# Means of squares of the second and third token group: block transposes on VectorE in place of matmuls, PSUM read out by ScalarE

## The chip, the cores and the metric

The kernel runs on one core of a Trainium2 chip. The metric is the device time of one execution in microseconds (us). The engines are named as in the profile: PE (TensorE's matmuls), PEld (its weight loads), DVE (VectorE), ACT (ScalarE), POOL (GpSimd) and SP (which only issues DMAs here). Each engine takes its instructions in program order; semaphores make one engine wait for another.

## What is computed

Attention without softmax, a normalisation of its result, and then two matrix products with a nonlinear function between them:

```python
kv = np.einsum('bhsd,bhse->bhde', k, v)                            # (8, 8, 64, 64)
out = np.einsum('bhsd,bhde->bhse', q, kv)                          # (8, 8, 576, 64)
rms = np.sqrt(np.mean(out * out, axis=-1, keepdims=True) + 1e-06)
x = (out / rms * g_norm)            # then (B,H,S,D) -> (B*S, H*D): 4608 x 512
h = x @ w_in                        # 4608 x 2048
g = h * erf(softplus(h))
result = g @ w_out                  # 4608 x 512
```

Everything is float32. What matters here is the third and the fourth line: a mean of squares over the 64 values of a head, for each token.

## The kernel before

**Groups and units.** The 8 batches of 576 tokens are worked on as nine groups of 512 tokens: the first 512 tokens of each batch are a group (T = 0 to 7), and the last 64 tokens of all batches together are the ninth. The hidden dimension of 2048 is cut into 16 units of 128. One loop (L1156) goes through n = 0 to 31, which are the units of the first group (n = 0 to 15) and of the second (n = 16 to 31); a second loop (L1323) does the other groups, four units at a time. While the units of one group are computed, the attention of the next one is prepared between them: that of the second group (T = 1) beside n = 0 to 15, and that of the third (T = 2, `FIRST`) beside n = 16 to 31. The attention of later groups is written differently (`paired`, L542) and the change only takes some of its lines out into functions of their own.

**Pairs.** A group's attention is done for two heads at a time, so in four pairs p = 0 to 3. `attention(T, p)` (L404) returns the steps of one pair and `pieces_of` (L1028) puts them into the iterations: every iteration has the places 3, 0, 1 and 2, in this order in time. For the second group the pairs begin at units f = 3, 6, 9 and 12, for the third at f = 0, 4, 8 and 12. Steps of a pair before the change:

- `visit` (in iteration f+1, place 1; for p = 0 of the second group f+2, place 3): PE multiplies q with k^T v of the pair into a PSUM tile of two banks, `at` (L427, L437), and k^T v of the *next* pair into another part of the same tile (L432). ACT squares the result `o` into `qT` (L445).
- `halve` and `keep_tail` (f+2, place 3): DVE splits the squares into an upper and a lower part (L459, L460; not for the first pair of the second group), copies the 64 last tokens' result into `x_last` (L448), and brings k^T v of the next pair into SBUF: each half of it is copied to the other half of the partitions (L371, two copies of 64 partitions) and added (L372).
- `mean` (f+2): PE multiplies the squares with a matrix of 1/64 (L470, L471; L476 for that first pair), so that the mean stands in every partition of its head, and ACT forms the reciprocal root over 128x512 values: Ln, Exp, Square (L482 to L484). ACT has to load its tables for Ln and Exp before (L114) and those for Softplus after them (L117), 1.28 us each.
- `norm` (f+3, place 0): DVE refines the root (L490, L493) and multiplies `o`, still in PSUM, with it (L502); `turn` (L347) transposes q of the next pair.
- `split` (f+4, place 0; third group): ACT and DVE cut x into the three parts that the next group's products take (L713, L716, L719).

For the last pair of the third group (p = 3, visit in n = 29), mean, norm and split come in `held_sums` (L1110), in n = 32, where the two loops meet. There PE also multiplies four units that were held back (`g_held`, L1098); DVE makes their parts (L716, L719) after `add` (L753) and `gates` (L1082) of unit n = 30, and PE waits for each part. The next unit's `n_ps` takes the PSUM tile that ACT has to empty first (L1216).

**What else is in the queues.** Beside n = 0 to 15 the weights, which come as 64-bit numbers, are made into float32: ACT takes the lower words (L271), DVE joins them in four operations (`w_join`, L281 to L292). The join of a pair of units has to be done before their first product (L1201). Beside n = 16 to 31 DVE and ACT cut all weights into three parts (`w_upper` L737, `w_lower` L740 and L743) and write them to memory. Every iteration also has, on ACT, the copy of the products out of PSUM (L1214, L1216) and Softplus (L1230), and on DVE `add` (second group, L753) and the product of h and erf (L1082).

**Two engines on one PSUM bank** take turns in program order, two readers too: DVE's first copy of `x_last` started at 46.16 us, when ACT's square of other columns of the same tile (45.55 us, 0.58 long) had ended, though PE had written these columns by 41.9 us.

Of the kernel before, what the change touches and what calls it, by code (L numbers as in the profile page):

```python
# [70 lines left out]
def kernel(  # L71
# [293 lines left out]
    def kv_kept(T, p, at, cols=kv_cols):  # L365


        kv = kv_of(T, p).rearrange("p (a e) -> p a e", a=2)
        other = other_tile(1)[:, 0]
        for i in range(2):  # L370
            nc.vector.tensor_copy(out=other[rows_of[i]], in_=at[rows_of[1 - i], ::-1, cols])  # L371
        nc.vector.tensor_tensor(out=kv, in0=at[:, :, cols], in1=other, op=ALU.add)  # L372
# [30 lines left out]

    def attention(T, p):  # L404
# [3 lines left out]
        halves = T > 1 or (T == 1 and p > 0)  # L408
# [7 lines left out]

        def square_tile(name):
            return qt_tile(name)[:, 0:G]

        def visit():  # L420
# [24 lines left out]
            nc.scalar.activation(two(st["sq"]), st["o"], AF.Square)  # L445

        def keep_tail():
            nc.vector.tensor_copy(  # L448
                out=x_last[:, p, T * R : T * R + R], in_=st["at"][:, 1, 2 * P : 2 * P + R]
            )  # L450
            kv_kept(*then, st["at"])
            if both:
                kv_kept(then[0], 1, st["at"], more_cols)

        def halve():
            sq = st.pop("sq")
            hi = st["hi"] = attp.tile([P, G], FP32R, name="sq_hi", tag="rms_r")
            lo = st["lo"] = attp.tile([P, G], FP32R, name="sq_lo", tag="sq_lo")
            nc.vector.tensor_copy(out=hi, in_=sq)  # L459
            nc.vector.tensor_tensor(out=lo, in0=sq, in1=hi.bitcast(FP32), op=ALU.subtract)  # L460

        def mean(table=True):
            ms = st["ms"] = st["at"][:, :, 2 * P : 4 * P]
            parts = [(ms[:, a], a) for a in range(2)]
            if halves:


                hi, lo = two(st.pop("hi")), two(st.pop("lo"))
                for ps, a in parts:
                    nc.tensor.matmul(ps, lhsT=mean_w, rhs=hi[:, a], start=True, stop=False)  # L470
                    nc.tensor.matmul(ps, lhsT=mean_w, rhs=lo[:, a], start=False, stop=True)  # L471
                u = square_tile("u")
            else:
                u = st.pop("sq")
                for ps, a in parts:
                    nc.tensor.matmul(  # L476
                        ps, lhsT=mean_w.bitcast(FP32), rhs=two(u)[:, a], start=True, stop=True
                    )
            r = attp.tile([P, G], FP32, name="rms_r", tag="rms_r")
            exp_ln_table()  # L480
            st["u"], st["r"] = u, r
            nc.scalar.activation(two(r), ms, AF.Ln, bias=eps_col)  # L482
            nc.scalar.activation(r, r, AF.Exp, scale=-0.5)
            nc.scalar.activation(u, r, AF.Square)  # L484
            if table:
                softplus_table()

        def norm():
            ms, u, r = (st.pop(name) for name in ("ms", "u", "r"))
            nc.vector.scalar_tensor_tensor(  # L490
                out=two(u), in0=ms, scalar=EPS, in1=two(u), op0=ALU.add, op1=ALU.mult
            )
            nc.vector.scalar_tensor_tensor(  # L493
                out=u, in0=u, scalar=3.0, in1=r, op0=ALU.subtract, op1=ALU.mult
            )
            if T < FIRST:
                if T not in xT:
                    xT[T] = wide.tile([P, KC, G], FP32, name="xT", tag="ab"[T])
                x = xT[T][:, p, :]
            else:  # L500
                x = st["x"] = x_new.tile([P, G], FP32, name="x", tag="x")
            nc.vector.scalar_tensor_tensor(  # L502
                out=two(x),
                in0=st.pop("o"),
                scalar=gm_col,
                in1=two(u),
                op0=ALU.mult,
                op1=ALU.mult,
            )

        def split_upper():
            if T >= FIRST:
                upper(st["x"], x_forms[T][0][:, p])

        def split_lower():
            if T >= FIRST:
                lower(st.pop("x"), *(form[:, p] for form in x_forms[T]))

        def split():
            split_upper()  # L520
            split_lower()
# [14 lines left out]
        pieces = (first_, (visit, loads), (halve, keep_tail) if halves else (keep_tail,))  # L536
        return (*(partial(chain, *group) for group in pieces), mean, partial(chain, norm, then_), split)
# [4 lines left out]
    def paired(T, p):  # L542
# [76 lines left out]
        def small(name):  # L619
            t = twice[name] = attp.tile([P, 2 * BLOCKS], FP32, name=name, tag=name)  # L620
            return t

        def block_sums():


            total = small("ms")
            for n in range(2):
                t = attp.tile([P, G], FP32, name="sq_t", tag=("rms_r", "sq_lo")[n])
                nc.vector.transpose(out=t, in_=twice["x"][n])
                nc.vector.tensor_reduce(  # L630
                    out=total[:, n * BLOCKS : n * BLOCKS + BLOCKS],
                    in_=t.rearrange("p (c d) -> p c d", c=BLOCKS),
                    axis=AX.X,
                    op=ALU.add,
                )

        def across():


            total, other = twice["ms"], small("ms_other")  # L640
            for n in range(4):
                rows, beside = (slice(32 * k, 32 * k + 32) for k in (n, n ^ 1))
                nc.scalar.copy(other[rows], total[beside])
            nc.vector.tensor_tensor(out=total, in0=total, in1=other, op=ALU.add)

        def root():
            total, r, u = twice["ms"], small("rms"), small("rms_u")
            exp_ln_table()
            nc.scalar.activation(r, total, AF.Ln, bias=eps_col)
            nc.scalar.activation(r, r, AF.Exp, scale=-0.5)  # L650
            nc.scalar.activation(u, r, AF.Square)
            softplus_table()

        def spread():


            total, r, u = (twice[name] for name in ("ms", "rms", "rms_u"))
            nc.vector.scalar_tensor_tensor(
                out=u, in0=total, scalar=EPS, in1=u, op0=ALU.add, op1=ALU.mult
            )  # L660
            nc.vector.scalar_tensor_tensor(
                out=u, in0=u, scalar=3.0, in1=r, op0=ALU.subtract, op1=ALU.mult
            )
            for n in range(2):
                nc.vector.transpose(
                    out=twice["x"][n].rearrange("p (c d) -> p c d", c=BLOCKS),
                    in_=u[:, n * BLOCKS : n * BLOCKS + BLOCKS].unsqueeze(2).to_broadcast([P, BLOCKS, 32]),
                )
# [783 lines left out]
```

## Time and profile before

| what | value |
|---|---|
| median of three runs | 884.97 us (883.99 to 885.11) |
| the profiled execution | 885.1 us, of which 883.2 us are its span |
| PE busy in the span | 875.2 us (99%), 4874 matmuls |
| DVE, ACT busy | 752.5 us (85%), 558.4 us (63%) |
| 51 to 116 us (second group's pairs 1 to 3): PE, DVE, ACT busy | 64.78, 61.80, 43.51 of 65.00 us |
| 129 to 216 us (third group's pairs): PE, DVE, ACT busy | 87.00, 75.78, 64.73 of 87.00 us |
| 216 to 250 us (`held_sums` and after): PE, DVE, ACT busy | 33.45, 29.87, 23.09 of 34.00 us |
| granted PE clock | 1.00 in all of these stretches |

The span is what the profiler's instructions cover; some 1.9 us of the execution lie around it. PE's time is modelled for the ends of its matmuls, so the starts are what to read: a row of matmuls without a gap between the starts is PE at work. DVE is nearly as full as PE while the second and third group are prepared, so an operation more on DVE may or may not be covered, and this has to be read place by place. In the views, each row has the start, the length, the engine and the line, and in brackets how long the engine had stood idle before it and what released it.

### The profile page before, as it was taken

The numbers are of one execution on the slowest core, as the hardware profiler recorded it, in microseconds if no ns is written. First come the engines' busy times: TensorE is split into PE (matmuls) and PEld (weight loads), VectorE is DVE, ScalarE is ACT, GpSimd is POOL, SyncE is SP. The second block draws the span as 40 slices with busy tenths as digits, with TensorE's granted clock in tenths as the row PEclk, the third lists the DMA queues.
The fourth block names the chain that finished last, engine by engine and source line by source line (L and its number), as shares of the span: only waits on it lengthen the run. The fifth ranks groups of instructions, "written<-read, shape, count | busy, mean of one in ns | idle before, by whom it ended". The sixth has DMA issues, their size and how long they took to land.

```text
span 883.2 us, 13302 instructions
## 1 busy us (share of the span) xinstructions
PE 875.2 (99%) x4874; PEld 656.1 (74%) x4874; DVE 752.5 (85%) x1107; ACT 558.4 (63%) x789; POOL 4.7 (1%) x14
## 2 busy tenths in 40 slices
PE   8999999999999999999999999999999999999998
PEld 4444456656788888888888888888888888888887
DVE  5889978899999898989898989898979797966667
ACT  5977677777775657565665647474757575755552
POOL 2000000000000000000000000000000000000000
PEclk9999999999999999999999999999999999999999
DMA  9967427989799997998799879998897778778861
GB/s 289 292 220 225 137 75 277 345 306 351 257 346 409 332 353 250 391 327 345 233 381 357 337 240 351 361 341 288 281 352 283 287 288 346 291 274 336 314 255 48
DMA packets 136929, 259.89 MB, mean 294 GB/s; under 512 B 78816, under 2 KB 87264, under 8 KB 136864
## 3 DMA queue, kind: packets, MB, share of 16 engines
q1 hardware_dynamic: 136128, 258.09, 81.8%
q10 hardware_dynamic: 544, 0.82, 0.3%
q8 instruction: 39, 0.64, 0.3%
q14 instruction: 26, 0.21, 0.1%
q0 software_dynamic: 192, 0.13, 0.0%
HBM read 224.40 MB, written 34.60 MB: 293 GB/s over the span
## 4 chain that ended last, share of the span: by engine, by line
PE 94%; DVE 2%; DMA 2%; ACT 1%; issue 0%; SPq 0%; DVEq 0%
PE n_ps L778 49%; PE m_ps L778 24%; PE o_ps L834 9%; PE h_ps L1201 5%; DMA w_out_parts<-w_out 1%; PE diag_ps L578 1%; PE at_ps L583 1%; PE n_ps L1098 1%; PE warm_ps L982 1%; DMA w_raw<-in_moe_w_out_dram 1%; PE at_ps L432 0%; PE at_ps L437 0%; PE o_ps L1098 0%; DVE w_in_sb L292 0%; DVE w_e L287 0%; PE off_ps L578 0%
## 5 line engine op out<-in xcount | busy, mean ns | idle before, releaser
L778 PE MATMUL n_ps<-w_out_parts,g_forms 128*128 128x512 f32 (+1 forms) x936 | 229.9, 388 | 0.2 <-DMA w_out_parts<-w_out 0.2
L778 PE MATMUL n_ps<-x_forms,w_in_parts 128*128 128x512 f32 x896 | 222.6, 390 | 0.0
L778 PEld LDWEIGHTS n_ps<-w_out_parts,g_forms 128*128 128x128 f32 x936 | 175.1, 188 | 36.5 <-DMA w_out_parts<-w_out 0.6
L778 PEld LDWEIGHTS n_ps<-x_forms,w_in_parts 128*128 128x128 f32 x896 | 167.4, 188 | 38.3 <-issue 3.9
L753 DVE TENSOR_TENSOR h<-m_ps,h 128x512 f32<-128x512 f32 x116 | 78.5, 686 | 66.1 <-PE m_ps L778 63.9
L1363 ACT ACTIVATE s<-h 128x512 f32<-128x512 f32 x112 | 69.2, 632 | 88.1 <-DVE h L753 88.1
L778 PE MATMUL m_ps<-w_out_parts,g_forms 128*128 128x512 f32 x464 | 123.9, 389 | 0.0
L1358 ACT ACTIVATE h<-n_ps 128x512 f32<-128x512 f32 x112 | 66.7, 596 | 85.6 <-PE n_ps L778 83.2
L778 PE MATMUL m_ps<-x_forms,w_in_parts 128*128 128x512 f32 x448 | 119.7, 389 | 0.0
L778 PEld LDWEIGHTS m_ps<-w_out_parts,g_forms 128*128 128x128 f32 x464 | 87.1, 188 | 18.1
L778 PEld LDWEIGHTS m_ps<-x_forms,w_in_parts 128*128 128x128 f32 x448 | 84.1, 188 | 17.5
L753 DVE TENSOR_TENSOR e<-m_ps,e 128x512 f32<-128x512 f32 x116 | 80.1, 691 | 13.8 <-PE m_ps L778 3.4
L834 PE MATMUL o_ps<-w_out_sb,h_sb 128*128 128x512 f32 x192 | 86.8, 595 | 0.0
L713 ACT ACTIVATE g_forms<-h 128x1024 fp32r<-128x1024 f32 x58 | 60.8, 1061 | 39.0 <-PE m_ps L778 20.8
L719 DVE SCALAR_TENSOR_TENSOR g_forms<-g_forms 128x1024 fp32r<-128x1024 f32 x58 | 71.1, 1225 | 2.0
L716 DVE TENSOR_TENSOR g_forms<-h,g_forms 128x1024 fp32r<-128x1024 f32 x58 | 70.5, 1216 | 0.5 <-ACT g_forms L713 0.4
L1412 DVE TENSOR_TENSOR h<-h,s 128x1024 f32<-128x1024 f32 x56 | 65.9, 1216 | 0.0
L834 PEld LDWEIGHTS o_ps<-w_out_sb,h_sb 128*128 128x128 f32 x192 | 35.5, 190 | 40.2 <-issue 38.0
L748 DVE SCALAR_TENSOR_TENSOR e<-n_ps,e 128x512 f32<-128x512 f32 (+1 forms) x89 | 59.8, 672 | 3.5 <-PE n_ps L778 3.5
L1201 PE MATMUL h_ps<-xT,w_in_sb 128*128 128x512 f32 x128 | 57.9, 596 | 1.3 <-DVE w_in_sb L292 1.2
L117 ACT ACT_TABLE_LOAD x43 | 55.2, 1283 | 0.8
L1386 ACT ACTIVATE s<-s 128x1024 f32<-128x1024 f32 x50 | 50.6, 1054 | 0.3
(166 smaller groups left out, 935.3 us busy)
## 6 DMA issues: line engine op xcount, KB each, us to landing
w_out_parts<-w_out SPq DMA_DIRECT2D x116, 768.0 KB, 7.2
w_in_parts<-w_in SPq DMA_DIRECT2D x112, 768.0 KB, 6.8
w_in<-w_new SPq DMA_DIRECT2D x16, 768.0 KB, 4.9
k_sb<-in_k_dram SPq DMA_DIRECT2D x32, 288.0 KB, 6.1
v_sb<-in_v_dram SPq DMA_DIRECT2D x31, 288.0 KB, 5.8
w_raw<-in_moe_w_in_dram SPq DMA_DIRECT2D x16, 512.0 KB, 6.2
w_raw<-in_moe_w_out_dram SPq DMA_DIRECT2D x8, 1024.0 KB, 5.0
out_dram<-e SPq DMA_DIRECT2D x32, 256.0 KB, 4.1
```

The source lines that it names most:

```text
L117: nc.scalar.preload_act_table_set("softplus")
L713: nc.scalar.activation(high, x, AF.Copy, scale=1.0 + 2.0**-13)
L716: nc.vector.tensor_tensor(out=low, in0=x, in1=high.bitcast(FP32), op=ALU.subtract)
L719: nc.vector.scalar_tensor_tensor(out=both, in0=low.bitcast(FP32), scalar=SHIFT, in1=high.bitcast(FP32), op0=ALU.mult, op1=ALU.add,)
L748: nc.vector.scalar_tensor_tensor(out=out_, in0=ps, scalar=scale, in1=out_, op0=ALU.mult, op1=ALU.add)
L753: nc.vector.tensor_tensor(out=out_, in0=ps, in1=out_, op=ALU.add)
L778: nc.tensor.matmul(ps[:, cols], lhsT=weights(form, k), rhs=moving(form, k)[:, cols], start=(form == forms[0] and k == 0), stop=(form == fo ...
L834: nc.tensor.matmul(o_ps[j], lhsT=g[:, j * P : j * P + P], rhs=one(w_out_sb, f), start=(f == 0), stop=last,)
L1201: nc.tensor.matmul(plain[i], lhsT=blocks_of(one(w_in_sb, i % FC))[:, c], rhs=xT[T][:, c, :], start=(c == 0), stop=(c == KC - 1),)
L1358: nc.scalar.activation(h[:, i], n_ps, AF.Copy, scale=SHIFT - 1.0)
L1363: nc.scalar.activation(s[:, i], h[:, i], AF.Softplus)
L1412: nc.vector.tensor_tensor(out=part(h, half), in0=part(h, half), in1=part(s, half), op=ALU.mult)
```

## The change

- The squares are no longer split and multiplied. DVE transposes them in blocks of 32x32 (`sums`) and adds up each block's rows, which gives 128x16 sums for a pair; `meet` then adds to each 32 partitions the sums of the 32 partitions beside them, by four copies on DVE and one addition. ACT's square has a scale of 0.125, so the sum is the mean.
- The root is taken of 128x16 or 128x32 values, and the pairs p = 0 and p = 1 of a group share one (`root`, `norm` and `split` of p = 0 do nothing but the `turn`, those of p = 1 do both pairs). Each of p = 2 and p = 3 has its own. `spread_over` brings the root back to 128x512 by a transpose.
- ACT copies `o` out of PSUM to where x will stand, copies the halves of k^T v to the other partitions, and copies the last tokens' result to `x_last`, all in `visit`. DVE keeps the addition (`kv_sum`).
- Where: `keep` and `sums` come in iteration f+1, place 2, after the products of the same iteration, where `halve` and `keep_tail` came in f+2, place 3; for p = 0 of the second group they stay in f+2, place 3. `root` is in f+2, place 1, `norm` in f+3 and `split` in f+4 as before.

```diff
+    def kv_beside(at, other, copy, cols=kv_cols):
+        for i in range(2):
+            copy(other[rows_of[i]], at[rows_of[1 - i], ::-1, cols])
+
+    def kv_sum(T, p, at, other, cols=kv_cols):
         kv = kv_of(T, p).rearrange("p (a e) -> p a e", a=2)
+        nc.vector.tensor_tensor(out=kv, in0=at[:, :, cols], in1=other, op=ALU.add)
...
+    def sum_blocks(total, n, t):
+        nc.vector.tensor_reduce(
+            out=total[:, n * BLOCKS : n * BLOCKS + BLOCKS],
+            in_=t.rearrange("p (c d) -> p c d", c=BLOCKS),
+            axis=AX.X,
+            op=ALU.add,
+        )
+
+    def meet(total, other, copy, n=2):
+        cols = slice(0, n * BLOCKS)
+        for k in range(4):
+            rows, beside = (slice(SQ * i, SQ * i + SQ) for i in (k, k ^ 1))
+            copy(other[rows, cols], total[beside, cols])
+        nc.vector.tensor_tensor(out=total[:, cols], in0=total[:, cols], in1=other[:, cols], op=ALU.add)
+
+    def roots(total, r, u, n=2):
+        total, r, u = (x[:, 0 : n * BLOCKS] for x in (total, r, u))
+        nc.scalar.activation(r, total, AF.Ln, bias=eps_col)
+        nc.scalar.activation(r, r, AF.Exp, scale=-0.5)
+        nc.scalar.activation(u, r, AF.Square)
+
+    def refine(total, r, u, n=2):
...
+    def spread_over(x, u, n):
+        nc.vector.transpose(
+            out=x.rearrange("p (c d) -> p c d", c=BLOCKS),
+            in_=u[:, n * BLOCKS : n * BLOCKS + BLOCKS].unsqueeze(2).to_broadcast([P, BLOCKS, SQ]),
+        )
...
-        halves = T > 1 or (T == 1 and p > 0)
+        alone = p > 1
...
             st["sq"] = qT[:, 0:G]
-            nc.scalar.activation(two(st["sq"]), st["o"], AF.Square)
...
+            nc.scalar.activation(two(st["sq"]), st["o"], AF.Square, scale=0.125)
...
+            st["x"] = x
+            nc.scalar.copy(two(x), st["o"])
+            others = st["others"] = other_tile(2)
+            kv_beside(at, others[:, 0], nc.scalar.copy)
+            if both:
+                kv_beside(at, others[:, 1], nc.scalar.copy, more_cols)
+            nc.scalar.copy(x_last[:, p, T * R : T * R + R], at[:, 1, 2 * P : 2 * P + R])
+
+        def keep():
+            others = st.pop("others")
+            kv_sum(*then, st["at"], others[:, 0])
+            if both:
+                kv_sum(then[0], 1, st["at"], others[:, 1], more_cols)
+
+        def sums():
...
+            t = attp.tile([P, G], FP32, name="sq_t", tag="rms_r")
+            nc.vector.transpose(out=t, in_=st["sq"])
+            sum_blocks(total, side, t)
+            shared[side] = st
+            if not alone and p == 0:
+                return
+            n = side + 1
+            other = small_tile("ms_other")
+            meet(total, other, nc.vector.tensor_copy, n)
+            st["n"] = n
+
+        def root(table=True):
+            if "n" not in st:
+                return
...
+        def norm():
+            if "n" not in st:
+                return
+            n = st["n"]
+            refine(st["ms"], st["r"], st["u"], n)
+            for i in range(n):
+                other = shared[i]
+                rb, x = other.pop("sq"), other["x"]
+                spread_over(rb, st["u"], i)
+                nc.vector.scalar_tensor_tensor(
+                    out=x, in0=x, scalar=gm_col, in1=rb, op0=ALU.mult, op1=ALU.mult
+                )
...
-        pieces = (first_, (visit, loads), (halve, keep_tail) if halves else (keep_tail,))
-        return (*(partial(chain, *group) for group in pieces), mean, partial(chain, norm, then_), split)
+        pieces = (first_, (visit, loads), (keep, sums))
+        return (*(partial(chain, *group) for group in pieces), root, partial(chain, norm, then_), split)
...
-            products, apply, halve, mean, norm, split = attention(T, p)
+            products, apply, after, mean, norm, split = attention(T, p)
...
-            steps[f][2 if T == FIRST or p == 1 else 1].append(products)
-            if T < FIRST and p == 0:
-                steps[f + 2][3].append(apply)
-            else:
-                steps[f + 1][1].append(apply)
-            steps[f + 2][3].append(halve)
+            first = T < FIRST and p == 0
+            steps[f][1].append(products)
+            steps[f + 2 if first else f + 1][3 if first else 1].append(apply)
+            steps[f + 2 if first else f + 1][3 if first else 2].append(after)
...
-            steps[f + 2][place].append(partial(mean, table=not with_erf))
+            steps[f + 2][1].append(partial(mean, table=not with_erf))
```

`products` is empty but for the first pair of the second group, whose place stays. `halve`, `keep_tail`, the old `mean` and the old `norm` go. The later groups' functions call `sum_blocks`, `meet` (there with ACT's copies), `roots`, `refine` and `spread_over` with the operations they had.

## The prediction

> **What bounds the kernel now.** I read the shares of the engines first, then the chain of waits, then the timelines of PE, DVE and ACT at the places that the change touches.
>
> ```profile
> PE 94%; DVE 2%; DMA 2%; ACT 1%; issue 0%; SPq 0%; DVEq 0%
> ```
>
> The chain is PE nearly everywhere, so a matmul less is worth its time where PE has no gap. From 51 to 216 us it has none. What the means cost there is read from the distance of two rows that are the same with and without them:
>
> ```profile
> 66.43 3.60 PE L1201 MATMUL h_ps<-xT,w_in_sb 128*128 128x512 f32 x8
> 69.46 0.68 PE L470 MATMUL at_ps<-sq_hi,mean_w 128*128 128x256 f32 x1
> ...
> 70.33 3.60 PE L834 MATMUL o_ps<-w_out_sb,h_sb 128*128 128x512 f32 x8
> 73.77 3.60 PE L1201 MATMUL h_ps<-xT,w_in_sb 128*128 128x512 f32 x8
> 77.20 3.60 PE L834 MATMUL o_ps<-w_out_sb,h_sb 128*128 128x512 f32 x8
> ```
>
> From L1201 to L834 it is 3.90 us with the four mean matmuls between and 3.43 us without. But PE's chain is broken at two places, and both times DVE, behind ACT, is what it waits for. The first is before unit 6 (PE's L1201 started at 51.22 us, after 0.50 us idle for L292):
>
> ```profile
> 45.55 0.58 ACT L445 ACTIVATE qT<-at_ps 128x512 f32<-128x512 f32 x1
> ...
> 46.02 1.13 ACT L271 ACTIVATE w_m<-w_raw 128x1024 int32<-128x1024 uint32 x1
> 46.16 0.23 DVE L448 COPY x_last<-at_ps 128x64 f32<-128x64 f32 x1 [1.84 <-ACT qT L445]
> ...
> 47.23 0.68 DVE L281 TENSOR_SCALAR w_e<-w_raw 128x1024 f32<-128x1024 f32 x1
> ...
> 49.94 1.22 DVE L292 CUSTOM_DVE_ANT_0 w_in_sb<-w_e,w_m 128x2048 uint16<-128x2048 uint16 x1
> ```
>
> The reader is to see one line of events: ACT's square, then DVE's small copies, then without a gap the join of unit 6's weights, then PE. Whatever is put between the square and L281 comes out at PE. The second is where the two loops meet:
>
> ```profile
> 216.79 0.60 ACT L445 ACTIVATE qT<-at_ps 128x512 f32<-128x512 f32 x1 [0.33 <-PE at_ps L437]
> ...
> 218.87 0.60 ACT L1216 ACTIVATE h<-n_ps 128x512 f32<-128x512 f32 x1 [0.44 <-PE n_ps L778]
> ...
> 220.51 0.68 DVE L753 TENSOR_TENSOR h<-m_ps,h 128x512 f32<-128x512 f32 x1
> ...
> 223.75 0.69 DVE L719 SCALAR_TENSOR_TENSOR g_held<-g_held 128x512 fp32r<-128x512 f32 x1
> ...
> 224.50 1.19 PE L1098 MATMUL o_ps<-w_place,g_held 128*128 128x512 f32 x4 [0.15 <-DVE g_held L719]
> ```
>
> DVE runs from 217.42 to 227.7 without a gap; PE's L1098 starts when L719 ends. What DVE gets before L753 comes out at PE here too. What follows (the matmuls of L1098, L1129, the last product of h and erf at 237.5, the loads of w_out_parts for which PE waits at 250.16) hangs on it.
>
> **Part 1, the matmuls that go.** Three pairs of the second group save 3.90 − 3.43 = 0.47 each; three of the third save 1.39 − 0.94 = 0.45 each (from the start of m_ps's four matmuls to L834's: 141.15 to 142.54 with means, 147.86 to 148.80 without). That is 2.76 us. The other two save nothing at once: p = 0 of the second group ends at 50.72, before PE waits for the join; the last pair's means (222.39) lie in front of the wait for g_held. PE is dense before and after the six, so they count in full: **−2.76**.
>
> **Part 2, p = 0 of the second group (46 to 51 us).** ACT gets three kinds of copies behind the square. Its o copy is like L1214 (128x512 out of PSUM, 0.58 long; the next operation starts 0.50 later). The copies of 64x128 and 128x64 are not in the trace on ACT: bounds are L643 (32x32, 0.216) and L1214 (0.58) each. On the straight line through these two rows, 128 columns are 0.29 and 64 columns 0.24, and I take these, the nearest DVE rows for the same shapes being 0.288 (L371) and 0.218 (L448). When the partitions change from one operation to the next there is no overlap (L643: four in 0.90), so 0.30 each. ACT: 46.02 + 0.50 + 0.60 + 0.25 = 47.37. `kv_sum` waits for all of it: for its copies as data, for x_last since that reads the same bank. DVE: 47.40, kv_sum 0.21 (L372 to L281), transpose 0.74 and reduction 0.60 (starts of L629, L630 and the next), so L281 at 48.95 instead of 47.23: **+1.72**. With ACT's bounds, 1.5 to 2.6. The relief in this pair (ACT's root and its two tables, 2 x 1.28 + 1.95; DVE's norm, 2.1) comes after the join and so can't help. L271 moves by 1.35, but the join of (out, 2) that needs it starts at 51.7.
>
> **Part 3, DVE while PE is dense.** Per pair DVE loses the split (0.46 + 0.61), x_last 0.23, the k^T v copies 0.62 and two of three norm operations (1.44): 3.36. It gains 1.34 (transpose, reduction), `meet`, refinement 0.43 and the transpose back 0.72. `meet` is four copies of 32 partitions. No row is that small: bounds are 0.10 (L644, 128x32, 252.29 to the next start 252.39) and 0.30 (L371). L644 itself is 0.184 long, and each copy changes the partitions, so I take 0.20: 0.8 and 0.2 for the addition, 3.5 in all. So DVE's work is about the same for p = 2 and 3 and some 1.4 less for p = 0 and 1 together; what grows is the waiting, since kv_sum stands behind 1.35 of ACT's copies and everything on DVE behind kv_sum. Beside n = 0 to 15 this is covered: PE takes each joined weight at least 3.4 us after L292 (in units 8: 63.05 to 66.43), and the closest product, gates at 81.40 for L834 at 85.33, has 3.2; I count it at nothing. Beside n = 16 to 31 the lag builds up from the third group's second pair on, in the trace's own time: +0.9 after p = 1 (kv_sum waits till 164.7, with sums and meet till 167.3 in place of 165.55, of which the idle 0.84 at 169.12 absorbs half; norm of two pairs 3.2 for 2.1), +1.3 for the second pair's split in the same iteration, −0.95 (idle at 188.33), +0.9 for p = 2's wait and work, −0.18 (idle at 195.90), −0.3 for its norm, −0.80 (idle at 215.11): **DVE is some 0.9 late at L753 of 215.11**. PE has to wait only if m_ps isn't emptied by the next unit's m_ps, some 3 us later: counted at nothing.
>
> **Part 4, the last pair (216 to 225 us).** Without the lag PE would be 2.76 − 1.72 = 1.04 early here; with it, ACT's Softplus waits for the late L753, and the square starts at about 215.83 + 0.9 + 0.57 = 217.3 instead of 216.79. On ACT: 217.3 + 0.47 + 0.50 + 4 x 0.31 (this pair has two k^T v) + 0.25 = 219.76. DVE: 219.8 + two kv_sum 0.5 + 0.74 + 0.63 + meet 0.8 + 0.2 = 222.67 at L753, before 220.51: **+2.15**. ACT's L1216, which PE's next n_ps waits for, goes from 218.87 to 220.8 (+1.9), a little less; the smaller root (Ln, Exp, Square 1.95 to 0.84) then ends before it is needed. So PE's L1098 at 224.50 comes at 226.65.
>
> **A rule of the Trainium skill.** Four DVE copies in a row are the change's new habit. Two copies of L371, whose partitions swap, take 0.59 for 2 x 0.288, while full 128x512 operations start 0.60 apart at a length of 0.69. "VectorE: DVE Perf Modes", section "Two Vector instructions with no wait between them", says why it speaks against the change: an instruction is held until all earlier ones have finished when its input or output starts in another quadrant of 32 partitions than the last one's. By the rule `meet` is the sum of four lengths, as taken; without it the copies would be some 0.1 apart, and the last part's sum 0.4 smaller.
>
> **Sum.** The end follows the DVE chain at L753, whose +2.15 already holds the gain of part 1 and the loss of part 2 (they only move PE, which waits here). 885.1 + 2.15 = 887.3 for a profiled execution; the median of the runs shown lies 0.13 below it: **887.2 us**. With the small copies at their bounds: `meet` at 0.10 a copy is −0.4 here and about −0.8 in the lag, 886.0; ACT's small copies at 0.58 and `meet` at 0.30 are +1.2 and +0.4 here and about +1.2 in the lag, 890.0.
>
> **Rivals.** About 0.2% (1.77 us) is what a measurement of this kernel can tell from no change, so the borders are 883.2 and 886.7.
>
> *The lag doesn't build up.* If DVE's idle pieces of 0.84 to 1.09 absorb each pair's wait, the square of the last pair starts with PE, 1.04 before 216.79 less the 0.33 that ACT waits there, and part 4 leaves 885.1 + 2.15 − 0.5 − 1.04 = 885.7. For it: four of the five gaps; against it: 1.3 us of one split moved into the iteration that has the least room (n = 24), and no gap over 0.2 between 189 and 215. 884.5 to 886.7: within 0.2%.
>
> *The copies run ahead (faster).* One mechanism: ACT, relieved of 2.6 us of tables and 1.95 of root in the first pairs and of 1.1 in each other root, does its copies while DVE is still at earlier work, so that kv_sum never waits. Then L281 comes at 47.2 or 47.7 and L753 of n = 30 no later than before, and 2.76 less up to 0.5 are left: 885.1 − 2.5 = 882.6. It decides from the point where the square at 45.55 could start 1.3 earlier. Against it: ACT has been busy without a gap from 37.3 to 45.55 with work that the change doesn't touch.
>
> *Dearer copies (slower still).* DVE's lag exceeds the 3 us to the next m_ps and PE waits inside units 25 to 29: over 889.9, up to 891.
>
> *It doesn't do what it says* only if the means stayed on PE; the diff leaves no L470 or L476 to run.
>
> **How the numbers follow.** Forecast and what lies near it, 886.7 to 889.9: 0.50. No lag, or only one of the two delays: 0.28. Copies ahead: 0.17. Dearer copies: 0.05. So faster 0.17, within 0.2% 0.28, slower 0.55. The range for 8 in 10 reaches from 882.9, which leaves out most of the rival that is faster, to the upper bound of 890.0.
>
> **What would show it.** In the changed kernel: no matmuls L470, L471, L476 and L1201 to L834 always 3.43 apart; PE idle for some 2 to 3 us before unit 6, released by L292; kv_sum on DVE idle behind ACT's x_last at every visit, by 1.3 more than L459 was; L753 of n = 30 (220.51) near 222.7; a gap of some 2 us on PE before n_ps of n = 31, released by L1216. The prediction is wrong if the gap before unit 6 stays at 0.5 (then copies cost nothing), if L753 of n = 30 comes before 220.5, or if PE has new gaps between 55 and 210.

## The result and the profile after

The change makes the kernel slower by half a per cent: **889.82 us** (median of six, 887.67 to 891.7) against 885.04 us (six, 883.99 to 885.37) on the same chip, ratio 1.0053, 95% interval 1.0037 to 1.0069. The profiled execution took 889.9 us with a span of 888.1; before it was 885.1 and 883.2. PE has 4842 matmuls where it had 4874 and is busy for 874.7 us, hardly less than the 875.2 of before. Of all the executions told below one, of 2252.29 us (of the kernel with the last pair late), is left out of the ratios.

The chain of waits of the kernel after, shares by engine:

```profile
PE 81%; DVE 8%; ACT 5%; DMA 3%; issue 2%; SPq 1%; DVEq 0%; ACTq 0%
```

It was PE for 94%. Followed back from PE's wait ahead of n = 31 (shown below), the chain now runs through DVE and ACT for much of the stretch from 60 to 222 us. What was to be saved is saved, as the timeline of PE in the second group shows (start, length, engine, line):

```profile
69.53 3.60 PE L1219 MATMUL h_ps<-xT,w_in_sb 128*128 128x512 f32 x8
72.97 3.60 PE L856 MATMUL o_ps<-w_out_sb,h_sb 128*128 128x512 f32 x8
76.40 3.60 PE L1219 MATMUL h_ps<-xT,w_in_sb 128*128 128x512 f32 x8
```

From L1219 to L856 it is 3.44 us, with no mean between, where it was 3.90. But this part starts late. Unit 6 in the timeline of all engines, after:

```profile
45.18 0.58 ACT L492 ACTIVATE qT<-at_ps 128x512 f32<-128x512 f32 x1
45.66 0.58 ACT L502 COPY xT<-at_ps 128x512 f32<-128x512 f32 x1
46.24 0.53 ACT L368 COPY kv_other<-at_ps 64x128 f32<-64x128 f32 x2
46.78 0.21 ACT L507 COPY x_last<-at_ps 128x64 f32<-128x64 f32 x1
47.03 0.29 DVE L372 TENSOR_TENSOR bd_kv<-at_ps,kv_other 128x128 f32<-128x128 f32 x1 [3.10 <-ACT x_last L507]
...
47.24 0.70 DVE L527 STREAM_TRANSPOSE sq_t<-qT 128x512 f32<-128x512 f32 x1
...
47.97 0.69 DVE L415 TENSOR_REDUCE ms<-sq_t 128x16 f32<-128x512 f32 x1
...
48.58 0.68 DVE L281 TENSOR_SCALAR w_e<-w_raw 128x1024 f32<-128x1024 f32 x1
...
51.28 1.22 DVE L292 CUSTOM_DVE_ANT_0 w_in_sb<-w_e,w_m 128x2048 uint16<-128x2048 uint16 x1
...
52.65 5.37 PE L1219 MATMUL h_ps<-xT,w_in_sb 128*128 128x512 f32 x8 [3.18 <-DVE w_in_sb L292]
```

Two things are to be seen. The join stands behind three kinds of ACT copies and three DVE operations, so PE waits 3.18 us where it waited 0.50. And the eight matmuls after the wait take 5.37 us instead of 3.60. Busy times of the same kernel by stretches (busy us and instructions of PE, its weight loads, DVE, ACT and POOL, then the granted clock of TensorE, DMA share, GB/s):

```profile
50.00:52.00 2.00, 0.00 (x0) 0.00 (x0) 1.94 (x2) 0.00 (x0) 0.00 (x0) 1.00 0.00 0
52.00:54.00 2.00, 1.35 (x3) 0.62 (x4) 1.97 (x4) 1.16 (x1) 0.00 (x0) 0.82 0.64 173
54.00:56.00 2.00, 2.00 (x4) 0.91 (x3) 1.83 (x3) 0.00 (x0) 0.00 (x0) 0.50 1.07 377
56.00:58.00 2.00, 2.00 (x5) 0.83 (x4) 2.00 (x3) 0.00 (x0) 0.00 (x0) 0.83 1.05 341
```

PE counts as busy, but half of its clock is withheld for 3.4 us (53.27 to 56.7 us in finer stretches). Where the loops meet, the timelines of ACT, PE and DVE of after, put together in order of time, have both again, a wait and a slower clock (0.63 us for a matmul of 0.40):

```profile
219.00 0.58 ACT L492 ACTIVATE qT<-at_ps 128x512 f32<-128x512 f32 x1
...
222.31 0.59 ACT L1234 ACTIVATE h<-n_ps 128x512 f32<-128x512 f32 x1
...
222.95 0.50 PE L800 MATMUL n_ps<-x_high,w_new 128*128 128x512 f32 x1 [1.79 <-ACT h L1234]
...
224.09 0.68 DVE L775 TENSOR_TENSOR h<-m_ps,h 128x512 f32<-128x512 f32 x1
...
224.42 0.63 PE L800 MATMUL n_ps<-x_low,w_new 128*128 128x512 f32 x1
...
225.70 1.85 PE L800 MATMUL m_ps<-x_both,w_new 128*128 128x512 f32 x4
...
254.75 0.73 PE L800 MATMUL n_ps<-w_out_parts,g_forms 128*128 128x512 f32 x2 [1.06 <-DMA w_out_parts<-w_out]
```

How late each event is against the kernel before, from the starts (the last column is the experiment e5_fill_short, told below):

| event | before | after | later by | short fill |
|---|---|---|---|---|
| unit 6, first product | 51.22 | 52.65 | +1.43 | 52.97 (+1.75) |
| next product of another line (L856) | 54.76 | 57.86 | +3.10 | 56.51 (+1.75) |
| `m_ps` of n = 29 | 213.90 | 215.01 | +1.11 | 213.66 (−0.24) |
| `add` of n = 30 (L775) | 220.51 | 224.09 | +3.58 | 222.75 (+2.24) |
| third group's first product | 235.13 | 238.83 | +3.70 | 237.39 (+2.26) |
| first `m_ps` after w_out_parts | 250.73 | 255.32 | +4.59 | 254.31 (+3.58) |
| span | 883.2 | 888.1 | +4.9 | 886.9 (+3.7) |

From 58 to 215 us the +3.10 shrinks to +1.11: that is the saved 2.76 us, less some 0.85 of small new waits (0.15 at 110 us, 0.31 at 128, 0.39 at 134). The last pair then loses it again, and the wait for w_out_parts grows from 0.18 to 1.06.

The second slow stretch costs next to nothing: `add` of n = 30 and the third group's first product are 3.58 and 3.70 late with it, 2.24 and 2.26 in the short fill, which has a wait of 1.61 there and no slow clock. Without it PE waits for DVE's parts of g_held instead (0.73 us in the short fill).

### The profile page after: what moved, and what is told of

It is laid out like the page before. It is cut to its first block, busy times and chain, and to the rows that moved or that the text cites. A ratio compares the mean times of both kernels' runs of the same rounds, so it can differ in the third digit from the quotient of the medians.

```text
span 888.1 us, 13265 instructions
## 1 busy us (share of the span) xinstructions
PE 874.7 (98%) x4842; PEld 653.7 (74%) x4842; DVE 750.4 (84%) x1117; ACT 551.8 (62%) x813; POOL 4.7 (1%) x14
## 4 chain that ended last, share of the span: by engine, by line
PE 81%; DVE 8%; ACT 5%; DMA 3%; issue 2%; SPq 1%; DVEq 0%; ACTq 0%
PE n_ps L800 48%; PE m_ps L800 24%; PE h_ps L1219 2%; PE o_ps L856 2%; DVE w_e L287 1%; DMA w_out_parts<-w_out 1%; PE diag_ps L623 1%; PE at_ps L628 1%; DVE w_e L284 1%; ACT s_sb L1172 1%; DVE w_e L281 1%; DVE h_sb L1100 1%; ACT L117 1%; PE warm_ps L1004 1%; DMA w_raw<-in_moe_w_out_dram 1%
## 5 line engine op out<-in xcount | busy, mean ns | idle before, releaser
L800 PE MATMUL n_ps<-x_forms,w_in_parts 128*128 128x512 f32 x896 | 222.7, 391 | 0.0
L775 DVE TENSOR_TENSOR h<-m_ps,h 128x512 f32<-128x512 f32 x116 | 78.5, 686 | 65.2 <-PE m_ps L800 65.1
L775 DVE TENSOR_TENSOR e<-m_ps,e 128x512 f32<-128x512 f32 x116 | 80.1, 692 | 14.2 <-PE m_ps L800 3.7
L856 PE MATMUL o_ps<-w_out_sb,h_sb 128*128 128x512 f32 x192 | 87.1, 596 | 0.1
L856 PEld LDWEIGHTS o_ps<-w_out_sb,h_sb 128*128 128x128 f32 x192 | 35.9, 190 | 42.4 <-issue 37.9
L1219 PE MATMUL h_ps<-xT,w_in_sb 128*128 128x512 f32 x128 | 59.5, 611 | 3.9 <-DVE w_in_sb L292 3.9
L1219 PEld LDWEIGHTS h_ps<-xT,w_in_sb 128*128 128x128 f32 x128 | 24.5, 195 | 36.1 <-issue 33.2
```

The source lines that it names most:

```text
L775: nc.vector.tensor_tensor(out=out_, in0=ps, in1=out_, op=ALU.add)
L800: nc.tensor.matmul(ps[:, cols], lhsT=weights(form, k), rhs=moving(form, k)[:, cols], start=(form == forms[0] and k == 0), stop=(form == fo ...
L856: nc.tensor.matmul(o_ps[j], lhsT=g[:, j * P : j * P + P], rhs=one(w_out_sb, f), start=(f == 0), stop=last,)
L1219: nc.tensor.matmul(plain[i], lhsT=blocks_of(one(w_in_sb, i % FC))[:, c], rhs=xT[T][:, c, :], start=(c == 0), stop=(c == KC - 1),)
```

## The experiments

**Theory A:** the change costs its two exposed waits (the join of unit 6, and the third group's last pair, ahead of n = 31), and the clock that falls when PE stands still. **Rivals:** B, the clock's fall has another cause or is off the path; C, the price is spread over the copies and transposes, or later waits hide it; D and E, what takes the place of the waits when they are gone (the root's chain, the load of w_out_parts); F, the price is the squares' transposes and block sums, whoever copies. Each kernel is given with its ratio to the kernel before on its own chip.

| kernel | ratio (95%) | span | gap before unit 6 | clock after it |
|---|---|---|---|---|
| after | 1.0053 (1.0037 to 1.0069) | 888.1 | 3.18 | 0.50 |
| first pair's sums late (e1_late_sums) | 0.9995 (0.9986 to 1.0004) | 882.2 | none | 1.00 |
| long fill (e2_fill_gap) | 1.0052 (1.0040 to 1.0064) | 889.3 | filled | 1.00 |
| short fill (e5_fill_short) | 1.0034 (1.0019 to 1.0048) | 886.9 | 0.52 left | 1.00 |
| last pair late (e3_late_copies) | 1.0041 (1.0025 to 1.0057) | 885.7 | 3.18 | 0.50 |
| both late (e4_both_late) | 0.9985 (0.9976 to 0.9994) | 882.2 | none | 1.00 |
| last pair spread (e8_ending_spread) | 0.9976 (0.9967 to 0.9986) | 882.0 | none | 1.00 |
| before, one operation more (e6_gap_one) | 1.0008 (0.9999 to 1.0016) | 883.2 | 1.24 | 1.00 |
| before, two more (e7_gap_two) | 1.0026 (1.0017 to 1.0034) | 886.1 | 1.96 | 1.00 |
| before, three more (e10_gap_three) | 1.0038 (1.0026 to 1.0051) | 887.9 | 2.70 | 0.50 |
| k^T v by VectorE (e9_kv_by_vector) | 1.0081 (1.0067 to 1.0095) | 887.9 | 3.15 | 0.50 |

### The first pair's sums behind the join

```
-            steps[f + 2 if first else f + 1][3 if first else 2].append(after)
+            steps[f + 2 if first else f + 1][2].append(after)
```

> The kernel after, with the first pair's kv_sum, transpose and block sums (2.0 us of VectorE) put at the end of unit 5's step, behind the join of unit 6's weights. Theory A (two exposed waits, and a TensorE clock that falls after a long one): unit 6's h_ps no longer waits 3.18 us but 0.5 or less, its clock stays at 1.00 and its eight matmuls take 3.6 us and not 5.37, so the end comes 2.7 + 1.7 = 4.4 us sooner, 885.4 us against 889.8; later small waits may keep 1 us of it back. Theory B (the wait costs, the clock does not depend on it): 2.7 us sooner, 887.1, with h_ps still near 5.4. Theory C (what costs is spread over the copies and transposes, and the end of the third group alone sets the time): less than 0.7 us sooner, above 889.1.

Measured: 0.9995, some 5.1 us under the kernel after; one line of placement takes the whole loss away. PE's timeline has no gap and no slow matmul at unit 6:

```profile
49.86 3.60 PE L1219 MATMUL h_ps<-xT,w_in_sb 128*128 128x512 f32 x8
53.29 3.60 PE L856 MATMUL o_ps<-w_out_sb,h_sb 128*128 128x512 f32 x8
```

Nothing downstream took it back: L856 comes 4.57 us sooner than after (57.86), the third group's first product 4.56 sooner (234.27). The rest of the difference of the spans lies behind that point, where PE did not wait for w_out_parts in this execution (1.06 us after). The wait ahead of n = 31 is still there, 1.58 us, without a slow clock. Theory C falls as it stands.

### PE kept at work in the gap

```
+            for _ in range(6 if n == 6 else 0):
+                nc.tensor.matmul(plain[n], lhsT=blocks_of(one(w_in_sb, 5))[:, 0],
+                                 rhs=xT[0][:, 0, :], start=True, stop=True)
```

The real products overwrite what these leave. First with six, then with three:

> The kernel after, with six more matmuls of 0.45 us put into unit 6's bank ahead of its own, which overwrite them: TensorE then works through 2.7 of the 3.18 us in which it waits for the join, and nothing else moves. Theory A (the clock falls because TensorE stands still): h_ps of unit 6 starts at the same time, 52.65, but takes 3.6 us at a clock of 1.00, and the end comes 1.7 us sooner, 888.1 against 889.8. Theory B (the clock's fall has another cause, or the time is lost elsewhere anyway): the clock in 52 to 58 us is again 0.5 to 0.8 and the time stays within 0.5 us of 889.8.

> The kernel after, with three more fp32 matmuls (six rows of about 0.43 us, 2.6 us in all) in unit 6's bank ahead of its own. The run with six of them filled 5.15 us, 2 us more than the gap, and so hid what it was to show. Theory A (the clock falls because TensorE stands still): unit 6's own matmuls start at the same time as in the kernel after, take 3.6 us at a clock of 1.00, and the end comes 1.7 us sooner than the kernel after (1.0053 of the kernel before): a ratio of 1.0034 or so, 888.0 us. Theory B (the time of the fallen clock is not on the path): within 0.5 us of the kernel after, 1.0048 to 1.0058.

The long fill says nothing by its time (1.0052): I had taken a row's 0.45 us for a whole fp32 matmul, but each is two rows, so it took 5.15 us. Its timeline, and that of the short fill below it:

```profile
49.89 5.31 PE L1219 MATMUL h_ps<-xT,w_in_sb 128*128 128x512 f32 x12
55.04 3.60 PE L1227 MATMUL h_ps<-xT,w_in_sb 128*128 128x512 f32 x8
```

```profile
49.71 2.74 PE L1219 MATMUL h_ps<-xT,w_in_sb 128*128 128x512 f32 x6
52.97 3.70 PE L1227 MATMUL h_ps<-xT,w_in_sb 128*128 128x512 f32 x8 [0.52 <-DVE w_in_sb L292]
56.51 3.60 PE L856 MATMUL o_ps<-w_out_sb,h_sb 128*128 128x512 f32 x8
```

With the short fill the join ends as late as in the kernel after, yet the matmuls take 3.70 us, L856 starts 1.35 us sooner, and the ratio is 1.0034, the number that theory A gave. By the ratios, useless matmuls make the kernel 1.7 us faster. The intervals overlap (1.0037 to 1.0069, 1.0019 to 1.0048), so the rows carry this more than the times do: in two kernels only the idle time was taken away, and the clock at unit 6 stayed at 1.00. Theory B falls.

### The last pair's copies and sums behind the held preparations

```
+            if (T, p) == (FIRST, NP - 1):
+                steps[f + 3][1].append(ending_copies[-1])
+                steps[f + 3][2].append(after)
...
```

`ending_copies` are the pair's o, k^T v and x_last copies, taken out of `visit`; all other pairs keep their place. Alone, then with the first edit:

> The kernel after, with the last pair's o, k^T v and x_last copies on ScalarE put behind unit 31's softplus instead of ahead of unit 30's copy of h, and its kv_sum, transpose, block sums and meeting on VectorE behind the last g_held parts. Theory A: unit 31's n_ps waits for nothing (1.79 us before), no slow clock follows it (0.9 us), the held products start by some 3.3 to 3.7 us sooner than at 227.39, the root of the last pair moves back to near 231 and is just in time for the third group's first products; the load of w_out_parts, issued after the last gates, comes sooner by as much. The end comes 3.7 to 4.6 us sooner, 885.2 to 886.1 against 889.8. Theory D (the root's chain takes the place of the waits): the first products of the third group wait 1 to 3 us for x_forms and the end comes less than 2.5 us sooner, above 887.3.

> Both moves together: the first pair's sums behind the join of unit 6's weights, and the last pair's copies and sums behind the held preparations. Theory A (the two waits are all that the change costs, and its seven saved groups of mean matmuls are a gain of 2.8 us of TensorE elsewhere): 4.4 + 3.7 to 4.6 us sooner, 881 to 882 us, faster than the kernel before (885.0) by 3 us. Theory C (the change also costs something spread over the groups): not below 884.

Alone it gives 1.0041, by the ratios some 1.1 us less than the kernel after; but the intervals overlap and its five executions lie between 885.8 and 890.8 us, so the times don't show a gain. The rows show why there is little of it, and theory D holds in part: the wait of 1.79 is gone, but a new one stands behind it, as ACT and PE of this kernel show:

```profile
230.94 0.31 ACT L433 ACTIVATE rms<-ms,eps_col 128x16 f32<-128x16 f32 x1 [1.62 <-DVE ms L429]
```

```profile
233.71 3.92 PE L1127 MATMUL n_ps<-w_place,g_held 128*128 128x512 f32 x16 [2.01 <-ACT e L1158]
```

ACT is in order: waiting for the late sums, it doesn't empty the first held sum, and PE waits for its bank. Both edits together give 0.9985, faster than the kernel before, though by 1.3 us and not by the 3 expected. The median, 883.7 us, is only just below the 884 of theory C, so a smaller price that is spread over the groups is not ruled out. What the rows show is that PE waits for the same ACT copy, and then for a DMA:

```profile
229.00 3.94 PE L1127 MATMUL n_ps<-w_place,g_held 128*128 128x512 f32 x16 [2.05 <-ACT e L1158]
...
249.14 0.73 PE L807 MATMUL n_ps<-w_out_parts,g_forms 128*128 128x512 f32 x2 [1.51 <-DMA w_out_parts<-w_out]
```

### The last pair's work taken apart

Square, transpose, sums and meeting stay; the o copy goes behind unit 31's Softplus, the other copies behind the root, kv_sum behind the forms.

```
+                steps[f + 3][1].append(ending_copies[0])
...
         mean()
+        ending_copies[1]()
...
         split()
+        ending_copies[2]()
```

`ending_copies` holds the o copy, the k^T v and x_last copies, and `keep`, in this order.

> The first pair's sums behind unit 6's join, as in e1_late_sums; and the last pair's work taken apart: its square, transpose, block sums and meeting stay where the kernel after has them, its o copy goes behind unit 31's softplus, its k^T v and x_last copies behind the root, and its kv_sum behind the third group's forms. In e4_both_late ScalarE waited 1.62 us for the sums at the root and TensorE therefore 2.05 us for the copy of the first held sum. Theory A: neither wait comes back, the third group's first product starts near 230.8 (232.8 in e4_both_late), the last gates and with them the load of w_out_parts some 2 us sooner, and the time is 881.7 us, ratio 0.9963. Theory E (the load of w_out_parts, some 13 us from the last gates to the last part, holds the end): no more than 0.7 us under e4_both_late, 0.998.

0.9976, the lowest ratio, 2.1 us under the kernel before (its interval overlaps that of both edits late). The root no longer waits (224.49) and PE's wait for the copy is 0.42. But the last gates come at 234.40 (234.62 with both edits simply late), so theory E is right about the rest:

```profile
228.58 3.94 PE L1127 MATMUL n_ps<-w_place,g_held 128*128 128x512 f32 x16 [0.42 <-ACT e L1159]
...
248.26 0.74 PE L810 MATMUL n_ps<-w_out_parts,g_forms 128*128 128x512 f32 x2 [1.04 <-DMA w_out_parts<-w_out]
```

The load was issued from 235.75 on, and PE goes on with its last part at 248.26; this wait of 1.04 us is the longest that PE has left behind 216 us.

### A gap in the kernel before, without the change

The first operation of unit 6's join is repeated (k = 1, 2, 3), which gives the same value again:

```
-        if late_:
+        for _ in range((1 + k * ((which, f) == ("in", 6))) if late_ else 0):
```

> The kernel before, without any part of the change, and with the first of the four VectorE operations of unit 6's join done twice (1.2 us more): TensorE's gap ahead of unit 6 grows from 0.50 to about 1.7 us. Theory A: the delay passes through to the end, 1.2 us, ratio 1.0014; the clock stays at 1.00 unless a gap under 2 us is enough, and where it is, 1.7 us come on top, 1.0033. Theory C (later waits take a delay at unit 6 back): under 0.5 us, 1.0005.

> The kernel before with that operation done three times (2.5 us more): a gap of about 3.0 us, nearly that of the kernel after (3.18). Theory A: 2.5 us of wait, and the clock falls to 0.5 for some 3.4 us after it, which loses 1.7 us more: 4.2 us in all, ratio 1.0047, close to the kernel after although no other part of the change is there. Theory B (the fall of the clock belongs to something else in the change): 2.5 us, 1.0028. Theory C (later waits take it back): under 1.0015.

> The kernel before with the first operation of unit 6's join done four times (some 3.6 us more): the runs with one and two more had gaps of 1.24 and 1.96 us and no fall of the clock in their profiles. Theory A: a gap of 3.0 to 3.9 us, as long as that of the kernel after, and a clock of 0.5 for some 3.4 us after it; the gap costs 2.5 to 3.4 us and the clock 1.7 us: ratio 1.0048 to 1.0058, as the kernel after. Theory B (the fall needs something else of the change): the gap alone, 1.0028 to 1.0038, and h_ps of unit 6 takes 3.6 to 3.7 us.

One operation lengthened the gap by only 0.74 us (the operation is 0.68 long, not 1.2 as I had it) and the end by about 0.7, in an interval that reaches down to no change; that a delay at unit 6 passes through to the end is shown by the two longer gaps. Two gave a gap of 1.96, in an execution in which PE arrived 1 us later, and no slower clock there; so it is no test of a gap of 3 us. Its +2.3 us are 0.9 more than two such operations (0.72 apart); six of its eleven executions have a mean clock of 0.998, where the kernel before has 0.999 or 1.000, so some may have had a slow stretch that the profile doesn't show. Three gave 2.70, and the clock fell with nothing of the change in the kernel:

```profile
52.90 5.40 PE L1201 MATMUL h_ps<-xT,w_in_sb 128*128 128x512 f32 x8 [2.70 <-DVE w_in_sb L292]
58.14 3.60 PE L834 MATMUL o_ps<-w_out_sb,h_sb 128*128 128x512 f32 x8
```

```profile
54.00:56.00 2.00, 2.00 (x4) 0.71 (x3) 1.93 (x3) 0.72 (x1) 0.00 (x0) 0.50 0.96 340
```

5.40 us for 3.60 again. The time, 1.0038 (3.4 us), lies between the ranges expected of the two theories, and a gap 2.2 us longer with 1.7 of clock (3.9) is within its interval; the mean clocks of its five executions go from 0.997 to 0.999, so some may have had no slow stretch. It is the row, and not the time, that decides for theory A.

### The k^T v halves copied by VectorE again

```
-            kv_beside(at, others[:, 0], nc.scalar.copy)
...
+            kv_beside(st["at"], others[:, 0], nc.vector.tensor_copy)
```

(The same for the second k^T v of the last pair, both moved from `visit` to `keep`.)

> The kernel after with one part of the change undone: VectorE copies the k^T v halves out of the bank, ahead of its kv_sum, as in the kernel before; the squares' transposes, the shared root and the o copies on ScalarE stay. Theory A with the copies on ScalarE as the larger half of its two waits: at unit 6 the kv_sum waits for no x_last (46.99), the two copies cost VectorE 0.57 us from about 45.0, the transpose can start when the square ends (45.7), and the join starts near 47.2 to 47.5 instead of 48.58: a gap of about 1.9 us instead of 3.18, and with it perhaps no fallen clock; at the last pair ScalarE's copy of unit 30's h comes 1.08 us sooner, and the gap ahead of unit 31 falls from 1.79 to about 0.7. Together 1.2 + 1.7 + 1.0 = 3.9 us sooner if the clock stays, 2.2 if not: ratio 1.0009 to 1.0028 against 1.0053. Rival F (the price is the squares' transposes and block sums in front of the join, whoever copies): under 1 us sooner, above 1.0042.

1.0081, by the ratios some 2.5 us slower still (the intervals just touch, and the profiled span is that of the kernel after), so ScalarE's copies are at least no loss: the gain that I expected from undoing them isn't there, and rival F stands. My expectation failed at its first step at unit 6. DVE's copies did not start at 45.0:

```profile
46.30 0.59 DVE L368 COPY kv_other<-at_ps 64x128 f32<-64x128 f32 x2 [2.45 <-ACT x_last L503]
```

They wait for ACT's last read of the same bank; the turns that two readers of a bank take, told above for the kernel before, I had left out. So the join starts at 48.48, the gap is 3.15, and DVE carries 1.2 us more at the last pair (`add` of n = 30 at 225.63). Ahead of n = 31 the gap did shrink, to 0.48, but PE then waits 1.02 us for `add` and 0.73 for g_held.

## Why the prediction was right, and what it lacked

The forecast was 887.2 us, in a range of 882.9 to 890.0, slower the likeliest. The sign, the two places and the mechanism of the two waits were right; the size was too small by 2.6 us. The measured 889.8 is 0.2 us below the upper end of the range, and that is luck: the range reached 890.0 by dearer small copies, and these were cheaper than taken; what filled it was the clock and a load.

- **Part 1** (−2.76): right. 2.84 us of lateness are worked off between 58 and 215 us if the small new waits are added back.
- **Part 2** (+1.72 at unit 6): right. In this execution everything ahead of it was 0.38 sooner (45.88 for 46.26 at L856), so the product came 1.43 + 0.38 = 1.81 later. The gap grew by more, 2.68, since the pair's own mean no longer fills 0.87 of it. The prices of the small copies were a little high (0.26 for a k^T v copy of 0.30, 0.21 for x_last at 0.25) and that of the o copy too low (0.58 for 0.50; the operations behind L1214 in the trace of before start 0.59 to 0.62 after it, not 0.50). From the square to L281 the errors cancel: 3.40 us, as forecast.
- **Part 3** (a lag of 0.9 on DVE, nothing on PE): DVE's `add` of n = 29 came 2.63 us later (217.74 for 215.11), of which 1.11 is PE's own delay; so the lag was 1.5. PE's small waits of 0.85 us, from 110 to 134 us, were counted at nothing.
- **Part 4** (+2.15 at `add` of n = 30): +3.58 in the kernel after, but +2.24 in the short fill, where the clock does not fall at unit 6. With the one thing taken away that the working left out, the term is right to 0.1 us, in part by luck: in the short fill `add` of n = 29 is 1.29 late (216.40) where 0.9 was forecast, and the pair itself adds 0.95 where 1.25 was.
- **The sum** is the step that failed: "they only move PE, which waits here" took a wait to cost its own length. A wait of 3.18 us also cost the clock, 5.37 − 3.60 = 1.77 us, and the granted clock of before (1.00 in every stretch) was read without asking what a longer gap does to it. The second term that it lacked is the load of w_out_parts: it was to move along with the gates, but it took 12.9 us from the first issue in the kernel after (241.86 to 254.75) and 11.9 in the kernel before (238.25 to 250.16). Its 0.9 us is on the path. The span grew by 4.9 us for the 2.15 of the sum: 1.34 of the difference are the clock (3.58 for 2.24), 0.9 the load, and 0.5 small terms.
- Of the rivals, "copies run ahead" never came: ACT was as full ahead of the square as the trace of before said. "Dearer copies" (over 889.9) gives nearly the measured time and is nevertheless wrong: the copies were cheaper than taken, and PE has no gap between units 25 and 29.
- **The signs:** the gap before unit 6, kv_sum behind x_last (14.1 us in six waits; the prediction had it at every one of the eight visits), and the gap before n = 31 released by ACT's copy of h are there. One of the signs of being wrong is there too, but small: PE has new gaps between 55 and 210 us, of 0.15 to 0.39. `add` of n = 30 was to be near 222.7; that it was at 224.09 pointed to what was missing.

Of the clock, "TensorE: Matmul & The Clock Gate" of the Trainium skill, section "Part 1: The HAM clock gate", says that an idle window of about 3.4 us halves the clock, that about 3.4 us of work bring it back, and that the window runs freely. The length agrees with these rows (3.4 us in the kernel after, with the last pair late and with three operations more), and so does the free-running window (last section). The threshold does not: gaps of 2.70 and 3.18, and of 1.79 at the second place, were followed by the half clock here. The page's rule of thumb would have let all of them pass.

Left open: why the first load of w_out_parts lands 11.9 to 13.6 us after its first issue where PE waits for it (11.9 before, 13.6 with the long fill).

## What to carry to other kernels

A step that only has to be done before a later iteration must not stand in the queue ahead of one that PE waits for: the same operations, put behind the join instead of ahead of it, turned +0.5% into nothing, and with the last pair taken apart into −0.24%. Price a new gap on PE by its length and by the half clock that can follow it (1.7 us at unit 6; next to nothing ahead of n = 31, where another wait took its place), and look for both in the rows: a PE that is busy may be running at half speed. Where an in-order engine serves two chains, ask for each moved step which other chain will stand behind it.

## What the runs showed of the hardware

- After a gap the granted clock stayed at 0.50 for 3.41 us each time it fell: 53.27 to 56.68 and 223.94 to 227.35 us (after), 52.16 to 55.58 (last pair late), 223.93 to 227.34 (long fill), 53.73 to 57.14 (k^T v by VectorE), 53.46 to 56.88 (three operations more). It began between 0.6 us before PE resumed (last pair late) and 1.2 us after (k^T v by VectorE).
- The length of the gap alone does not decide; the idle time of PE within one window of a fixed grid does. In every profile the times from one change of the granted clock to the next are whole multiples of 3.413 us (in the kernel after 47.79, 3.41 and 167.25 us, which are 14, 1 and 49 of them). Windows of this length, laid over PE's rows from these changes:

| gap | window (us) | PE idle in it | clock in the next window |
|---|---|---|---|
| 3.18, after | 49.86 to 53.27 | 2.80 | 0.50 |
| 2.70, three operations more | 50.05 to 53.46 | 2.70 | 0.50 |
| 3.18, last pair late | 48.75 to 52.16 | 2.62 | 0.50 |
| 3.15, k^T v by VectorE | 50.31 to 53.73 | 2.24 | 0.50 |
| 1.85 ahead of n = 31, long fill | 220.52 to 223.93 | 1.85 | 0.50 |
| 1.79 ahead of n = 31, after | 220.52 to 223.94 | 1.80 | 0.50 |
| 1.61 ahead of n = 31, short fill | 219.97 to 223.39 | 1.62 | 1.00 |
| 1.96, two operations more | 49.63 to 53.04, and the next | 1.33 and 0.63 | 1.00 |
| 2.01 for the held sum, last pair late | 229.66 to 233.07, and the next | 1.37 and 0.64 | 1.00 |
| 2.05 for the held sum, both late | 224.52 to 227.94, and the next | 0.99 and 1.06 | 1.00 |

  From the first full clock to 880 us the twelve profiles have no other window with more than 1.62 us of idle PE, and no other fall of the clock. So the gaps of 1.79 and 1.85 us, each inside one window, halved the clock, and those of 1.96 to 2.05, shared by two, did not. An estimate from these rows: a gap of up to 1.62 us alone does not halve the clock, one of twice 1.80 us or more always does, and in between it depends on where the grid falls. No run here has a value between 1.62 and 1.80.
- One such stretch lowers the mean clock of an execution by 0.002 (half of 3.4 us in 885). The six executions of the kernel after have mean clocks of 0.995 to 0.998, the eleven with the first pair's sums late 0.999 to 1.000. The times of the six do not follow it (887.67 us at 0.997, 891.7 at 0.998), so the 4 us between them have another cause, which stays open.
- ACT's small copies out of PSUM are cheap: 0.26 us for 64x128 and 0.21 for 128x64, where a copy of 128x512 takes 0.58. Four DVE copies of 32x16, each to other partitions, take 0.70 us together and four of 32x32 0.73, at 0.16 to 0.18 each: they do not overlap, as the prediction took it.
